# Score products of a transformer block on one Trainium2 core: 64-row tile pairs in every step with fillers

## The chip, the cores and the metric

The kernel runs on one core of one Trainium2 chip. The metric is the device time of one execution in microseconds (us); lower is better. A core has five engines that each work through their own instruction queue in order: PE (TensorE, matrix products into PSUM), DVE (VectorE), ACT (ScalarE), POOL (GpSimd) and SP (SyncE, which here only issues DMAs). They meet through semaphores.

## What is computed

One transformer block over 2048 rows of width 512, in bf16: layer norm, attention with 32 heads of width 16, a residual, layer norm, a gated feed-forward layer of width 1792, a residual.

```python
B, S, D, H, F = 1, 2048, 512, 32, 1792
q, k, v = split_heads(layernorm(x) @ wqkv)          # Dh = 16
p = softmax(einsum("bhqd,bhkd->bhqk", q, k) * Dh ** -0.5)
h = x + merge_heads(einsum("bhqk,bhkd->bhqd", p, v)) @ wo
g, u = layernorm(h) @ w_gate, layernorm(h) @ w_up
out = h + (sigmoid(g) * u) @ w_down
```

## The kernel before

**Tiling.** Queries are cut into five chunks, three of 512 and two of 256 (`CHUNKS`, L43). Within a chunk `c`, heads go in eight groups `g` of four heads `j`. A unit (`units`, L390) is one head against one bank's worth of keys: 128 keys by 512 queries, or twice 128 keys by 256 queries in the last two chunks. Three units in a row make a step (`groups`, L391, `GU = 3`); there are 683 steps `i`. Four steps are a cycle (`CYC = 4`); below, "step 0 to 3 of a cycle" is `i % 4`.

**A step.** `emit_scores(i)` (L746) issues the step's score products on PE into one of two PSUM buffers of three banks, `pss2[i % 2]`: three matmuls with 512 columns, or six with 256. Then ACT takes the exponential of the three tiles in one instruction (L776) and writes it to SBUF. In a split step (`split`, L898: step 0 of each cycle, and step 2 of the cycles that are in `twice`, L899 to L905) ACT takes two tiles and DVE the third, by a chain of a bit conversion that reads PSUM (`exp_bits`, L795) and four more operations in the steps that follow (L798 to L808). Scores of step `i` must wait until ACT, and DVE in a split step, have read the same buffer in step `i - 2`.

**What else PE does in a step.** After the scores stand, in this order: the products of exponentials with values that are due (`emit_pv`, L839: 12 matmuls of 17 columns of weights, most often in step 2 of a cycle), work put off by `later` (the normalisation by the row sums, loads), and then the fillers. Fillers are the other matrix products of the block (projections, output projection, feed-forward), written as one generator `filler` (L724) from which `emit_fill` (L861) takes a number of matmuls each step: `rate` (L737) allows 2 to 3 of full size in steps 0, 1 and 3 of a cycle, none where values are due. Fillers also pause: a `yield ("gap", n)` or `("at", n)` in the generator sets `state["wait"]`, the step at which they go on, to leave time for the DVE or ACT work on their result. The order on every engine is this program order.

**Two ways to write a score product.** `KT` holds 128 rows for a group of four heads: 32 rows a head, of which 16 carry the keys and the other 16 carry ones for a bound. `QB` (per head) is zero outside the head's own rows. So a product over all 128 rows gives one head's scores, and so does a product over the 64 rows in which the head lies (heads 0 and 1 in rows 0 to 63, heads 2 and 3 in rows 64 to 127). With `pairs` the 64 rows are used, with a tile position (L764 to L767); two such matmuls in different halves can run in PE side by side. Where the first two units of a step lie in the same half, `order` (L753, L754) turns the second and third round, so that the first two matmuls always lie in different halves; the third stands alone.

**Who has pairs now.** All steps before step 44 (`FIRST`); after that the odd steps, and all four steps of a cycle in `twice`. `idle` (L750) marks steps 0 and 1 of a cycle, from step 132 on, in a stretch in which the fillers are finished or wait past the next cycle; those steps have no pairs.

Of the kernel before, what the change touches and what calls it, by code (L numbers as in the profile page):

```python
# [18 lines left out]
def kernel(  # L19
# [27 lines left out]
    CYC = 4  # L47
    RATES = ((2.0, 2.0, 0.0, 3.0), (2.0, 2.5, 0.0, 3.0))
    FIRST = 44
# [165 lines left out]
    def emit_q_rows(n):  # L215
        c, g = qgs[n]
        q0, w = CHUNKS[c]
        assert ("q", q0 // QC, g // 2) in ready
        for j in range(4):
            r = 64 * (g % 2) + DH * j  # L220
            nc.sync.dma_start(out=QB[n % 2][32 * j:32 * j + 32:2, j, 0:w],
                              in_=QTu[r:r + DH, g // 2, q0:q0 + w])

    def emit_q_bound(n, engs=(nc.sync, nc.sync)):
        c, g = qgs[n]
        q0, w = CHUNKS[c]
        qc, o = q0 // QC, q0 % QC
        assert ("b", qc, g // 2) in ready
        r = 32 * qc + 4 * g
        for h in range(2):  # L230
            engs[h].dma_start(out=QB[n % 2][64 * h + 1:64 * h + 2, 2 * h:2 * h + 2, 0:w],
                              in_=bnd[r + 2 * h:r + 2 * h + 2, o:o + w])
# [151 lines left out]
    def per_bank(c):  # L384
        return QC // CHUNKS[c][1]
# [360 lines left out]
    def emit_scores(i):  # L746
        group = groups[i]
        n = len(group)
        pss = pss2[i % 2]
        idle = i >= 3 * FIRST and i % CYC < 2 and (state["done"] or state["wait"] > i + CYC)  # L750
        pairs = i < FIRST or (i % 2 == 1 or i - i % CYC + 2 in twice) and not idle
        order = list(enumerate(group))
        if pairs and group[0][3] // 2 == group[1][3] // 2:  # L753
            order[1:] = order[:0:-1]  # L754
        n_of = max(per_bank(u[0]) for u in group)
        parts = [(ui, u, h) for h in range(n_of) for ui, u in order[:2] if h < per_bank(u[0])]
        parts += [(ui, u, h) for ui, u in order[2:] for h in range(per_bank(u[0]))]
        for ui, (c, g, k, j), h in parts:
            n_qg = c * NG + g
            w = CHUNKS[c][1]  # L760
            kt = k * per_bank(c) + h
            assert ("k", g // 2) in ready
            h0 = 64 * (j // 2)
            rows = slice(h0, h0 + 64) if pairs else slice(0, P)  # L764
            nc.tensor.matmul(pss[:, ui, h * w:(h + 1) * w], lhsT=KT[rows, g, kt * P:(kt + 1) * P],  # L765
                             rhs=QB[n_qg % 2][rows, j, 0:w], start=True, stop=True,
                             tile_position=(h0, 0) if pairs else None)  # L767
        for c, g, k, j in group:
            n_qg = c * NG + g
            if k == (12 if per_bank(c) == 1 else 0) and j == 3 and n_qg + 1 < len(qgs):  # L770
                emit_q_rows(n_qg + 1)
                emit_q_bound(n_qg + 1)
        slot = i % 7
        pt = pt4[slot] if slot < 4 else (pt_early if i < GM else pt_late)[slot - 4]
        na = n - 1 if i in split else n
        ex = nc.scalar.activation(out=pt[:, 0:na, :], in_=pss[:, 0:na, :], func=ACT.Exp, scale=DH ** -0.5 / QS)  # L776
        if na < n:
            scratch = scratch_of(i)
            tc.declare_no_dep(exp_bits(pss[:, na, :], *scratch).ins, ex.ins,
                              reason="both only read, from different banks")  # L780
            later(i + 1, lambda: exp_first(*scratch))
            later(i + 2, lambda: exp_second(*scratch))
            later(i + 3, lambda: exp_third(pt[:, na, :], *scratch))
        for ui, u in enumerate(group):
            p_of[u] = pt[:, ui, :]

    def scratch_of(i):
        if i % CYC:
            flat = OT[(int((i - 20) / SPC) + 1) % 2][:].rearrange("p g q -> p (g q)")
            return (flat[:, 0:2 * QC].bitcast(mybir.dt.int32), flat[:, 2 * QC:4 * QC].bitcast(mybir.dt.int32),  # L790
                    flat[:, 4 * QC:6 * QC].bitcast(FP32))
        return early_scratch if i < GM else late_scratch

    def exp_bits(src, e_bits, e_man, e_pol):
        return nc.vector.tensor_scalar(out=e_bits, in0=src, scalar1=ONE_BITS, scalar2=0.0, op0=ALU.add, op1=ALU.max)  # L795

    def exp_first(e_bits, e_man, e_pol):
        nc.vector.tensor_scalar(out=e_man, in0=e_bits, scalar1=0x7FFFFF, scalar2=-0x40800000,  # L798
                                op0=ALU.bitwise_and, op1=ALU.bitwise_or)
        m = e_man.bitcast(FP32)  # L800
        nc.vector.scalar_tensor_tensor(out=e_pol, in0=m, scalar=PA, in1=m, op0=ALU.add, op1=ALU.mult)  # L801

    def exp_second(e_bits, e_man, e_pol):
        nc.vector.scalar_tensor_tensor(out=e_pol, in0=e_pol, scalar=PB, in1=e_man.bitcast(FP32),  # L804
                                       op0=ALU.add, op1=ALU.mult)

    def exp_third(dst, e_bits, e_man, e_pol):
        nc.vector.scalar_tensor_tensor(out=dst, in0=e_pol, scalar=PC, in1=e_bits.bitcast(FP32),  # L808
                                       op0=ALU.add, op1=ALU.mult)
# [44 lines left out]
    def later(i, fn):  # L854
        due.setdefault(i, []).append(fn)
# [43 lines left out]
    twice = set()  # L899
# [24 lines left out]
    with tc.manual_schedule():  # L924
# [17 lines left out]
        for i in range(NS + LAG):  # L942
            if i < NS:
                emit_scores(i)
            for u in pv_due.pop(i, []):
                emit_pv(*u[:3], i)
            for fn in due.pop(i, []):
                fn()
            if 1 <= i < NS:
                emit_fill(i)  # L950
# [37 lines left out]
```

## Time and profile before

| | |
|---|---|
| median of 3 runs | 966.58 us (966.09 to 969.06) |
| the profiled execution, its own time | 967.7 us |
| its span, first to last instruction | 965.9 us |
| mean granted PE clock in it | 0.996 of full speed |
| ACT busy | 897.1 us (93%) |
| PE busy | 837.0 us (87%), 6409 matmuls |
| DVE busy | 788.7 us (82%) |
| exponentials on ACT (L776) | 683 instructions, 882.8 us |
| score products (L765) | 2560 matmuls, 473.2 us |

A group row reads: line, engine, operation, output<-inputs, partitions by elements and type, count | busy time, mean ns of one | idle time of the engine just before, with what ended it. For matmuls "64\*128" is the rows and columns of the weights. Matmuls are pipelined and their ends are modelled, so starts are the better measure of PE: what one matmul costs is the time to the start of the next.

The timeline reads: start, length, engine, line, operation, and how many instructions are merged in the row; in brackets the idle time before it and what ended it. A row of three merged matmuls lasts until the modelled end of the third. The windows view gives, for a stretch of the span, the busy time of an engine, the granted PE clock (1.00 is full speed) and DMA.

### The profile page before, as it was taken

The page shows a single profiled execution, that of the slowest core. Times are in us where ns is not written, and L with a number is a line of the kernel's source. Part 1 is how long each engine was busy: PE and PEld are TensorE (multiplying, and loading weights), DVE is VectorE, ACT ScalarE, POOL GpSimd, SP SyncE. Part 2 cuts the span into 40 slices and gives each one's busy share as a digit, 9 for nine tenths or more (in the row PEclk, how much of TensorE's full clock was granted, in tenths as well). Part 3 has the DMA queues.
Part 4 walks back from the last instruction along what each step waited for, and adds up shares of the span by engine and source line. Part 5 has one row for each costly group of instructions (what it writes and reads, how often), then busy time and mean ns, then how long its engine had stood idle before and what let it go on. Part 6 is the DMA issues. An engine that isn't in the chain of part 4 may idle for free.

```text
span 965.9 us, 17209 instructions
## 1 busy us (share of the span) xinstructions
PE 837.0 (87%) x6409; PEld 334.2 (35%) x6409; DVE 788.7 (82%) x1423; ACT 897.1 (93%) x770; POOL 39.0 (4%) x45
## 2 busy tenths in 40 slices
PE   4888888888889899988789999988788999998988
PEld 2221222222223232222222233222255555456646
DVE  8389999888888888898888888888898788777653
ACT  4799999999999999999999999989998999899862
POOL 4600000000000000000000000000000000000000
PEclk9999999999999999999999999999999999999999
DMA  5002341000003000001000000000010000110010
GB/s 161 20 1 56 114 95 38 15 15 3 15 26 103 15 15 16 16 12 27 15 26 27 16 16 16 12 17 26 16 29 24 16 12 13 27 32 16 9 35 12
DMA packets 37357, 28.39 MB, mean 29 GB/s; under 512 B 17692, under 2 KB 32632, under 8 KB 37272
## 3 DMA queue, kind: packets, MB, share of 16 engines
q1 hardware_dynamic: 35684, 25.71, 10.1%
q10 hardware_dynamic: 1588, 1.58, 0.5%
q8 instruction: 50, 0.82, 0.4%
q14 instruction: 35, 0.29, 0.1%
HBM read 20.31 MB, written 2.61 MB: 24 GB/s over the span
## 4 chain that ended last, share of the span: by engine, by line
PE 41%; DVE 26%; ACT 24%; issue 6%; DMA 2%; SPq 0%; ACTq 0%; DVEq 0%; POOL 0%
PE pss L765 20%; ACT pt L776 13%; PE acc L846 8%; PE pm L514 6%; ACT stg L776 4%; ACT wd L776 4%; DVE stg L795 3%; PE pm L530 3%; ACT QTu L776 2%; PE pm L490 2%; DVE st L137 2%; DVE reg L798 2%; DVE pt L808 2%; DVE y L801 2%; DVE y L804 2%
## 5 line engine op out<-in xcount | busy, mean ns | idle before, releaser
L765 PE MATMUL pss<-QB,KT 64*128 64x512 bf16 (+3 forms) x2560 | 473.2, 338 | 85.7 <-ACT pt L776 40.1
L776 ACT ACTIVATE pt<-pss 128x1536 bf16<-128x1536 f32 (+1 forms) x392 | 500.4, 1360 | 18.1 <-PE pss L765 14.8
L765 PEld LDWEIGHTS <-KT 64*128 64x128 bf16 (+1 forms) x2560 | 179.0, 95 | 345.4 <-issue 235.2
L776 ACT ACTIVATE stg<-pss 128x1536 bf16<-128x1536 f32 (+1 forms) x140 | 183.1, 1356 | 5.0 <-PE pss L765 4.2
L795 DVE TENSOR_SCALAR stg<-pss 128x512 int32<-128x512 f32 x123 | 84.8, 689 | 72.4 <-PE pss L765 60.5
L846 PE MATMUL acc<-pt,Vaug 128*17 128x512 bf16 (+1 forms) x1471 | 112.8, 339 | 5.8 <-DVE xs_all L820 3.7
L776 ACT ACTIVATE wd<-pss 128x1536 bf16<-128x1536 f32 (+1 forms) x80 | 103.8, 1392 | 1.4 <-PE pss L765 1.3
L776 ACT ACTIVATE QTu<-pss 128x1024 bf16<-128x1024 f32 (+1 forms) x71 | 95.5, 1345 | 1.7 <-PE pss L765 1.2
L801 DVE SCALAR_TENSOR_TENSOR y<-reg 128x512 f32<-128x512 f32 x123 | 85.2, 692 | 4.2
L804 DVE SCALAR_TENSOR_TENSOR y<-y,reg 128x512 f32<-128x512 f32 x123 | 84.2, 685 | 1.1
L846 PEld LDWEIGHTS <-Vaug 128*17 128x17 bf16 x2560 | 50.4, 89 | 97.4 <-issue 82.6
L530 PE MATMUL pm<-wd,reg 128*128 128x512 bf16 x224 | 62.4, 385 | 2.3 <-DVE ob L535 1.8
L514 PE MATMUL pm<-reg,reg 128*128 128x512 bf16 (+1 forms) x280 | 58.0, 337 | 6.4 <-DVE reg L527 6.2
L514 PE MATMUL pm<-reg,wu 128*128 128x512 bf16 (+1 forms) x280 | 58.1, 338 | 1.5 <-ACT sg L519 1.2
L798 DVE TENSOR_SCALAR reg<-stg 128x512 int32<-128x512 int32 x123 | 52.0, 423 | 2.0
L144 POOL TENSOR_TENSOR rs<-ve,pw_neg 128x1 f32<-128x1 f32 (+1 forms) x24 | 16.5, 687 | 894.5 <-DVE ve L142 893.9
L846 PE MATMUL acc<-stg,Vaug 128*17 128x256 bf16 (+1 forms) x564 | 50.7, 326 | 0.8 <-DVE stg L808 0.4
L527 DVE SCALAR_TENSOR_TENSOR reg<-sg,pm 128x512 bf16<-128x512 f32 x56 | 38.2, 683 | 14.5 <-PE pm L514 13.8
L808 DVE SCALAR_TENSOR_TENSOR pt<-y,stg 128x512 bf16<-128x512 f32 x70 | 47.8, 683 | 1.8
L519 ACT ACTIVATE sg<-pm 128x512 f32<-128x512 f32 x56 | 35.5, 633 | 10.3 <-PE pm L514 10.0
L795 DVE TENSOR_SCALAR wd<-pss 128x512 int32<-128x512 f32 x45 | 30.9, 687 | 13.0 <-PE pss L765 12.7
L163 PE MATMUL pm<-reg 128*128 128x512 bf16 x124 | 37.1, 387 | 1.2 <-DVE km L171 0.7
(115 smaller groups left out, 707.0 us busy)
## 6 DMA issues: line engine op xcount, KB each, us to landing
rb_all<-rd SPq DMA_DIRECT2D x96, 64.0 KB
reg<-in_A_x_dram SPq DMA_DIRECT2D x8, 256.0 KB
xr<-in_A_x_dram SPq DMA_DIRECT2D x16, 128.0 KB
out_dram<-ob SPq DMA_DIRECT2D x16, 128.0 KB
rb_all<-rd SPq DMA_DIRECT2D x60, 32.0 KB
KT<-stg SPq DMA_DIRECT2D x7, 256.0 KB
reg<-in_B_w_gate_dram SPq DMA_DIRECT2D x4, 448.0 KB
wu<-in_B_w_up_dram SPq DMA_DIRECT2D x4, 448.0 KB
```

The lines of the kernel that those rows point to most:

```text
L163: nc.tensor.matmul(ps[:], lhsT=wqkv_sb[:, c, w0:w0 + P], rhs=xnT[:, c, n * QC:(n + 1) * QC], start=(c == 0), stop=(c == DC - 1))
L514: nc.tensor.matmul(ps[:, i * w:(i + 1) * w], lhsT=wt[:, c, f * P:(f + 1) * P], rhs=hnT[:, c, 0:w], start=(c == 0), stop=(c == DC - 1))
L527: nc.vector.scalar_tensor_tensor(out=out, in0=a, scalar=1.0, in1=b, op0=ALU.add, op1=ALU.mult)
L530: nc.tensor.matmul(ps[:], lhsT=hT[:, f, tt * P:(tt + 1) * P], rhs=wd[:, f, :], start=(f == 0), stop=(f == FC - 1))
L765: nc.tensor.matmul(pss[:, ui, h * w:(h + 1) * w], lhsT=KT[rows, g, kt * P:(kt + 1) * P], rhs=QB[n_qg % 2][rows, j, 0:w], start=True, stop= ...
L776: ex = nc.scalar.activation(out=pt[:, 0:na, :], in_=pss[:, 0:na, :], func=ACT.Exp, scale=DH ** -0.5 / QS)
L795: return nc.vector.tensor_scalar(out=e_bits, in0=src, scalar1=ONE_BITS, scalar2=0.0, op0=ALU.add, op1=ALU.max)
L798: nc.vector.tensor_scalar(out=e_man, in0=e_bits, scalar1=0x7FFFFF, scalar2=-0x40800000, op0=ALU.bitwise_and, op1=ALU.bitwise_or)
L801: nc.vector.scalar_tensor_tensor(out=e_pol, in0=m, scalar=PA, in1=m, op0=ALU.add, op1=ALU.mult)
L804: nc.vector.scalar_tensor_tensor(out=e_pol, in0=e_pol, scalar=PB, in1=e_man.bitcast(FP32), op0=ALU.add, op1=ALU.mult)
L808: nc.vector.scalar_tensor_tensor(out=dst, in0=e_pol, scalar=PC, in1=e_bits.bitcast(FP32), op0=ALU.add, op1=ALU.mult)
L846: nc.tensor.matmul(acc[32 * j:32 * j + VW, 0:w], lhsT=Vaug[:, kt, 4 * g + j, :], rhs=p[:, h * w:(h + 1) * w], start=(kt == 0), stop=(kt == ...
```

## The change

One condition in `emit_scores` is changed. Before, a step from 44 on has pairs if it is odd or its cycle is in `twice`, and it isn't idle. After, every step has pairs that isn't idle.

```diff
         idle = i >= 3 * FIRST and i % CYC < 2 and (state["done"] or state["wait"] > i + CYC)
-        pairs = i < FIRST or (i % 2 == 1 or i - i % CYC + 2 in twice) and not idle
+        pairs = i < FIRST or not idle
         order = list(enumerate(group))
         if pairs and group[0][3] // 2 == group[1][3] // 2:
             order[1:] = order[:0:-1]
...
             rows = slice(h0, h0 + 64) if pairs else slice(0, P)
             nc.tensor.matmul(pss[:, ui, h * w:(h + 1) * w], lhsT=KT[rows, g, kt * P:(kt + 1) * P],
                              rhs=QB[n_qg % 2][rows, j, 0:w], start=True, stop=True,
                              tile_position=(h0, 0) if pairs else None)
```

It reaches 266 of the 683 steps: 129 that are step 0 of a cycle and 137 that are step 2. The 24 idle steps (12 of step 0, 12 of step 1) stay as they are. The number of instructions on each engine, the step in which each filler stands and the queues of ACT, DVE, POOL and SP stay the same; on PE the score matmuls of these steps change form, and some of them change places within their step.

## The prediction, made before the changed kernel was run

> **What bounds the kernel now.** I read the head of the page first, then ACT's groups by form, then what waits for the score line, then the timeline of single steps, last the granted clock.
>
> ```profile
> span 965.9 us, 17209 instructions
> PE 837.0 (87%) x6409; PEld 334.2 (35%) x6409; DVE 788.7 (82%) x1423; ACT 897.1 (93%) x770; POOL 39.0 (4%) x45
> ```
>
> ```profile
> L776 ACT ACTIVATE pt<-pss 128x1536 bf16<-128x1536 f32 x281 | 400.3, 1479 | 12.0 <-PE pss L765 9.2 <-issue 1.2 <-DVE y L801 0.6
> L776 ACT ACTIVATE stg<-pss 128x1536 bf16<-128x1536 f32 x100 | 144.4, 1477 | 3.6 <-PE pss L765 3.1 <-ACT pt L776 0.2
> L776 ACT ACTIVATE pt<-pss 128x1024 bf16<-128x1024 f32 x111 | 117.5, 1058 | 6.1 <-PE pss L765 5.6
> ```
>
> ```profile
> who waited for it (us, times):
>   DVE stg L795: 60.5, 59
>   ACT pt L776: 14.8, 29
> ```
>
> ACT is the bound: its chain of exponentials fills the span from 36 to 933 us. In the timeline two exponentials of 1536 that follow each other without delay start 1.331 us apart (the records overlap by some 0.12), and after one of 1024 the next starts 0.905 later. What PE can win is only what ACT waits for it. I went through the timeline and took, for every exponential from step 44 on, how much later it starts than 0.11 us before the end of ACT's instruction ahead of it; counting delays over 0.06 us, 95 exponentials are late by 30.0 us together: 31 of unpaired step 0 by 10.8 us, 23 of unpaired step 2 by 6.2, 31 of step 1 by 10.3, ten others by 2.7. Of the 10.8, one delay alone is 2.8 (below).
>
> **The price of a pair.** The timeline around 402 us has both forms between fillers:
>
> ```profile
> 402.43 0.81 PE L765 MATMUL pss<-QB,KT 128*128 128x512 bf16 x3
> 403.08 0.59 PE L530 MATMUL pm<-wd,reg 128*128 128x512 bf16 x2
> 403.60 0.61 PE L765 MATMUL pss<-QB,KT 64*128 64x512 bf16 x3
> ...
> 406.45 0.82 PE L530 MATMUL pm<-wd,reg 128*128 128x512 bf16 x3
> 407.20 0.60 PE L765 MATMUL pss<-QB,KT 64*128 64x512 bf16 x3
> 407.74 0.39 PE L530 MATMUL pm<-wd,reg 128*128 128x512 bf16 x1
> ```
>
> Unpaired scores hold PE for 403.08 - 402.43 = 0.65 us, three slots of 0.216. Paired they take two slots, since the first two matmuls start 3 to 4 ns apart. But the last filler ahead of them holds PE for 403.60 - 403.08 - 0.216 = 0.30 us instead of 0.216 (over the trace the median is 0.312), and the last score matmul ahead of a filler holds it for 0.308 (407.74 - 407.20 = 0.54 = 0.23 + 0.31). So each change between 128-row, 64-row and 17-column forms costs about 0.093 us. Between 256-column matmuls it is the same: 0.109 becomes 0.202 to 0.205.
>
> The 266 changed steps each lose one slot, 0.215 us (0.204 in the 76 with six matmuls of 256 columns): -56.3 us of PE time. The form changes follow from PE's neighbours. Step 0: 44 have fillers on both sides (+2 each), 59 fillers ahead and paired scores behind (+1 - 1), 21 paired scores on both sides (-2), the other five come out at 0. Step 2, always followed by value products: 97 have a filler ahead (+1), 40 paired scores (-1). Sum 88 - 42 + 97 - 40 = +103, x 0.093 = +9.6 us. PE is relieved of 46.7 us, most of which turns into PE's own waiting.
>
> For a step's own scores: they are ready 0.215 - 0.093 = 0.12 us earlier behind fillers (200 steps) and 0.31 earlier behind scores (64). Steps 0 and 2 follow an exponential of 1.331, while buffer release to exponential takes an unpaired step 0.05 + 0.43 + 0.47 = 0.95 us, so nothing is won where PE was free.
>
> **What of it reaches ACT.** From each late exponential I went back along PE until PE was idle, summing what the change takes off or adds on the way, no more than the delay. Unpaired step 0 gets back 3.9 us, step 2 3.6, step 1 0.7: 8.2 us, the lower bound; it lets every wait at which a walk ends stand. The upper bound comes from the 42 steps 0 and 2 of cycles in `twice`, paired already: late by 0.34 us together, 8 ns each. If all 266 became like these, the 17.0 us of steps 0 and 2 would shrink to 2.1; without the 2.8 that is 12.1. I take **-10 us**. The other delays hang on fillers that wait for DVE (step 1 of the last two chunks) and stay. ACT, DVE, SP and POOL have the same queues, no wait is added, and no step's DMAs move.
>
> **The clock.** The price on the other side is in the granted clock.
>
> ```profile
> 644.27:647.68 3.41, 2.27 (x13) 1.00 0.02 5
> 647.68:651.10 3.42, 3.13 (x14) 0.54 0.02 4
> ```
>
> ```profile
> 646.40 0.61 PE L765 MATMUL pss<-QB,KT 64*128 64x512 bf16 x3 [0.27 <-ACT stg L776]
> ...
> 647.97 1.03 PE L846 MATMUL acc<-pt,Vaug 128*17 128x512 bf16 x8 [0.96 <-DVE xs_all L820]
> ...
> 648.93 1.46 PE L530 MATMUL pm<-wd,reg 128*128 128x512 bf16 x3
> 650.19 1.40 PE L765 MATMUL pss<-QB,KT 128*128 128x512 bf16 x3
> ...
> 651.69 5.09 ACT L776 ACTIVATE pt<-pss 128x1024 bf16<-128x1024 f32 x4 [2.65 <-PE pss L765]
> ```
>
> From 647.7 us the clock was halved for 3.41 us (three fillers take 1.26 instead of 0.65) and ACT stood for 2.65. The other halving inside the kernel starts at 36.7 us, 179 times 3.413 earlier: so the clock is judged in fixed stretches of 3.41 us. I counted in each how long any matmul streams (columns x 0.42 ns from its start, overlaps once). The stretch ahead of 647.7 had 41%; all the others between 40 and 930 us that did not bring a halving had 45% or more. So the limit lies between. The change takes 0.215 us, 6% of such a stretch, out for every changed step in it. The thin places are steps 3, 0, 1 without fillers:
>
> ```profile
> 195.38 0.81 PE L765 MATMUL pss<-QB,KT 128*128 128x512 bf16 x3 [0.58 <-ACT pt L776]
> 196.73 0.61 PE L765 MATMUL pss<-QB,KT 64*128 64x512 bf16 x3 [0.54 <-ACT wd L776]
> 197.65 0.81 PE L765 MATMUL pss<-QB,KT 128*128 128x512 bf16 x3 [0.31 <-ACT wd L776]
> 198.38 0.81 PE L846 MATMUL acc<-pt,Vaug 128*17 128x512 bf16 x9
> ```
>
> There 43% becomes 31%. Laying the 3.41 us grid at every phase over the trace, I count before 0.7 stretches under 41% and 2.7 under 45%, after 5.3 and 9.7: some 22 places, each hit in a quarter of the phases on average. I take **5 more halvings**.
>
> What does one cost? Here, halved from 197.65: scores take 0.43 more instead of 0.65 in all, so the step's exponential is still in time; the 12 value products take 1.3 and their form changes 0.19 each, so step 3's scores start near 200.2 instead of 199.14. Its exponential, due at 200.11, then comes 0.8 (clock back) to 1.3 us late. The halving seen cost 2.8, of which some 1.1 was the wait on L820. Bounds 0.8 and 2.8; most thin places are like this one, so 1.2 each: **+6 us**.
>
> [...]
>
> **Sum.** 967.7 - 10 + 6 = 963.7 against the profiled execution (span 965.9 and 1.8 around it). That one lies 1.1 above the median of the runs, and I carry the offset over: **962.6 us**.
>
> **Rivals.**
> - *The clock decides (slower).* The limit is at 45% or above, and a halving falls on fillers: 9 more at 1.7 (2.8 less 1.1) = 15.3, gain 8.2: 966.6 + 7.1 = 973.7. From 5 more at 1.7, or 7 at 1.2, the gain is gone. For it: the 31% places lie far under any limit, and value products follow them. Against: each place needs the grid to fall right.
> - *The clock stays.* Paired tiles may count as more work, and only a stretch without any matmul may bring a halving: 966.6 - 10 = 956.6. For it: in the first 44 steps, all paired, a stretch of 45% at 74 us brought none. Against: 647.7. [...]
> - *Little reaches ACT.* If the delays hang on DVE and the fillers' waits, walks gain some 3 us (a third of 8.2), the halvings 5: 966.6 + 2 = 968.6. For it: 22.6 of the 30 us come after 531 us, where fillers wait for DVE most. Against: the 42 paired steps.
> - That the change does not do what it says I leave out: the form is set on the matmul itself.
>
> **Chances.** Forecast 0.42 (own range 959 to 967), clock decides 0.28, clock stays 0.15, little reaches ACT 0.15. The range runs from 955 (gain 12.1, no halving) to 974. A measurement here tells about 0.3% (2.9 us) from no change. Faster than 963.7: 0.28 of the forecast and all of the clock that stays, 0.43. Within: 0.14 of the forecast, 0.11 of the third rival, 0.03 of the first, 0.28. Slower: 0.29.
>
> **What would show it.** Right: score rows of even steps in the 64-row form with 0.31 us at their edges; unpaired L765 only in idle steps; ACT's idle time on L765 down by a third or more; four to eight rows of clock near 0.5, mostly ahead of value products behind stretches without fillers, each with ACT late by about a microsecond. Wrong: no halving, or more than nine; ACT's instructions longer while two tiles write PSUM; delays of steps 0 and 2 unchanged.

## The result and the profile after

| | before | after |
|---|---|---|
| median of the runs | 966.81 us (966.09 to 970.78, 8 runs) | 977.27 us (969.57 to 982.88, 8 runs) |
| ratio of times | | 1.0101, 95% interval 1.0066 to 1.0136 |
| profiled execution, own time and span | 967.7 and 965.9 us | 979.0 and 977.2 us |
| mean granted PE clock, profiled execution | 0.996 | 0.970 |
| mean granted PE clock, 8 runs of after | | 0.965 to 0.982 |

The changed kernel is about 1% slower, and its runs differ from each other by 13 us, where those before differ by 5. The 962.6 us forecast, and the range up to 974, were wrong.

The head of the page after the change, and its row of the granted clock in 40 slices (tenths of full speed):

```profile
span 977.2 us, 17106 instructions
PE 812.0 (83%) x6313; PEld 282.7 (29%) x6409; DVE 789.4 (81%) x1423; ACT 897.1 (92%) x770; POOL 39.0 (4%) x45
...
PEclk9898999998989999999999999999999999999999
```

ACT is busy for the same 897.1 us, so its instructions did not get longer while two tiles write PSUM. (This trace lacks 96 of the 6409 matmul records, so PE's busy time can't be compared closely.) The new thing is the 8 in the clock row, in four slices. Before, the row was:

```profile
PEclk9999999999999999999999999999999999999999
```

ACT's groups by form, and what waits for the score line:

```profile
L776 ACT ACTIVATE pt<-pss 128x1536 bf16<-128x1536 f32 x281 | 401.0, 1483 | 18.9 <-PE pss L765 15.2 <-ACT pt L776 1.6 <-issue 1.1
L776 ACT ACTIVATE stg<-pss 128x1536 bf16<-128x1536 f32 x100 | 144.7, 1484 | 4.4 <-PE pss L765 3.0 <-ACT stg L776 0.7 <-ACT pt L776 0.3
```

```profile
who waited for it (us, times):
  DVE stg L795: 57.5, 58
  ACT pt L776: 21.4, 33
```

The exponentials wait 15.2 us for the scores in the first group where it was 9.2, though nearly all score products now have the cheaper form. The timeline shows that form, now in a step 0 between fillers:

```profile
406.64 0.81 PE L530 MATMUL pm<-wd,reg 128*128 128x512 bf16 x2 [0.59 <-DVE reg L527]
407.38 0.60 PE L765 MATMUL pss<-QB,KT 64*128 64x512 bf16 x3
407.91 0.61 PE L530 MATMUL pm<-wd,reg 128*128 128x512 bf16 x2
408.45 1.29 PE L765 MATMUL pss<-QB,KT 64*128 64x512 bf16 x6
```

From 407.38 to 407.91 the scores hold PE for 0.53 us, as forecast (0.23 + 0.31), where the 128-row form took 0.65; the fillers behind them for 0.54, two slots of 0.216 and 0.1 for the change of form.

Where the time went is seen in the windows view and the timeline around 240 us, in a stretch without fillers. Columns of the windows: stretch, its length, busy time and count of PE, PEld, DVE, ACT, POOL, then the granted clock. (The windows were laid some 0.2 us ahead of the recorded switches of the clock, hence 0.53 and 0.97 at the ends of the halving.)

```profile
235.20:238.65 3.45, 1.70 (x9) 0.39 (x8) 2.48 (x4) 3.45 (x4) 0.00 (x0) 1.00 0.00 0
238.65:242.07 3.42, 2.56 (x18) 0.65 (x19) 1.98 (x3) 3.42 (x3) 0.00 (x0) 0.53 0.01 2
242.07:245.48 3.41, 3.41 (x11) 0.47 (x11) 1.81 (x3) 1.53 (x3) 0.00 (x0) 0.50 0.03 5
245.48:248.89 3.41, 3.41 (x19) 0.59 (x20) 2.58 (x5) 2.46 (x3) 0.00 (x0) 0.50 0.03 2
248.89:252.30 3.41, 3.10 (x21) 0.82 (x23) 1.90 (x4) 3.38 (x3) 0.00 (x0) 0.97 0.31 84
```

```profile
238.15 0.59 PE L765 MATMUL pss<-QB,KT 64*128 64x512 bf16 x3 [0.31 <-ACT wd L776]
...
239.50 1.04 PE L765 MATMUL pss<-QB,KT 64*128 64x512 bf16 x3 [0.39 <-ACT wd L776]
240.46 1.02 PE L846 MATMUL acc<-pt,Vaug 128*17 128x512 bf16 x5
...
241.97 1.03 PE L765 MATMUL pss<-QB,KT 64*128 64x512 bf16 x3 [0.47 <-issue]
...
243.10 1.02 ACT L776 ACTIVATE pt<-pss 128x1024 bf16<-128x1024 f32 x1 [0.97 <-PE pss L765]
...
245.03 1.45 ACT L776 ACTIVATE pt<-pss 128x1536 bf16<-128x1536 f32 x1 [0.91 <-PE pss L765]
...
248.89 2.50 ACT L776 ACTIVATE wd<-pss 128x1536 bf16<-128x1536 f32 x2 [0.90 <-PE pss L765]
```

After a thin stretch (nine matmuls) the clock is halved for three stretches of 3.41 us, the scores' row grows from 0.59 to 1.04, and ACT stands three times for 0.9 us or a little more. In two of the halved stretches PE reads as busy for all of 3.41 us: the busy column alone would call this a full engine.

I took the delays of the exponentials apart once more, in the same way as in the prediction, from step 44 on:

| us of delay of the exponentials | before | after |
|---|---|---|
| in or up to 1.5 us behind a halved stretch | 2.8 (1 stretch of 3.41 us) | 17.5 (15 stretches in 12 groups, one of them before step 44) |
| elsewhere | 27.3 | 20.8 |

By this split the pairs did bring 6.5 us, and the clock took 14.7. The other 3 us of the 11.3 between the spans lie before step 44, in steps that are the same in both kernels: there the clock was halved at 37.5 us for two stretches (one before the change), and at 85.3 us for two. How much is halved differs from run to run, as the mean clock of 0.965 to 0.982 shows.

The runs say the same without a trace. Each comes with its mean clock, so the time at half clock is (1 - mean clock) x 2 x time (the clock records of both traces have 1.0 and 0.5 alone). Over the 8 runs after, the time grows by 0.37 us per halved us (correlation 0.96), over 24 runs before by 0.30 (0.93). Drawn out to no halving, this gives **957.7 us after and 965.8 before**: at full clock the change gains some 8.1 us. The 957.7 lies far from the runs, all of which have some 35 us or more at half clock, and its standard error is 2.2 us. On average after had 53.1 us at half clock and before 4.9, 14 stretches more, each worth 0.37 x 3.41 = 1.26 us.

### The profile page after: what moved, and what is told of

It reads as the page before. It is cut to its first block, busy times and chain, and to the rows that moved or that the text cites. A ratio compares the mean times of both kernels' runs of the same rounds, so it can differ in the third digit from the quotient of the medians.

```text
span 977.2 us, 17106 instructions
## 1 busy us (share of the span) xinstructions
PE 812.0 (83%) x6313; PEld 282.7 (29%) x6409; DVE 789.4 (81%) x1423; ACT 897.1 (92%) x770; POOL 39.0 (4%) x45
## 4 chain that ended last, share of the span: by engine, by line
PE 39%; DVE 27%; ACT 23%; issue 6%; DMA 2%; SPq 1%; ACTq 0%; POOL 0%; DVEq 0%
PE pss L765 18%; ACT pt L776 12%; PE acc L846 7%; PE pm L514 6%; ACT stg L776 4%; ACT wd L776 4%; DVE stg L795 3%; PE pm L530 3%; DVE pt L808 2%; ACT QTu L776 2%; DVE st L137 2%; DVE y L804 2%; DVE reg L798 2%; DVE y L801 1%; PE pm L490 1%
## 5 line engine op out<-in xcount | busy, mean ns | idle before, releaser
L765 PE MATMUL pss<-QB,KT 64*128 64x512 bf16 (+3 forms) x2555 | 425.5, 345 | 109.4 <-ACT pt L776 51.3
L765 PEld LDWEIGHTS <-KT 64*128 64x128 bf16 (+1 forms) x2560 | 128.0, 94 | 384.2 <-issue 311.5
L846 PE MATMUL acc<-pt,Vaug 128*17 128x512 bf16 (+1 forms) x1471 | 117.6, 350 | 6.5 <-DVE xs_all L820 3.3
L530 PE MATMUL pm<-wd,reg 128*128 128x512 bf16 x200 | 58.6, 388 | 5.9 <-issue 3.2
L514 PE MATMUL pm<-reg,reg 128*128 128x512 bf16 (+1 forms) x252 | 55.6, 333 | 8.8 <-DVE reg L527 6.7
L519 ACT ACTIVATE sg<-pm 128x512 f32<-128x512 f32 x56 | 36.3, 647 | 10.5 <-PE pm L514 10.5
L163 PE MATMUL pm<-reg 128*128 128x512 bf16 x106 | 35.4, 406 | 3.2 <-issue 1.7
```

The costliest lines, as they stand in the source:

```text
L514: nc.tensor.matmul(ps[:, i * w:(i + 1) * w], lhsT=wt[:, c, f * P:(f + 1) * P], rhs=hnT[:, c, 0:w], start=(c == 0), stop=(c == DC - 1))
L519: nc.scalar.activation(out=sg[:], in_=ps[:], func=ACT.Tanh, scale=0.5)
L530: nc.tensor.matmul(ps[:], lhsT=hT[:, f, tt * P:(tt + 1) * P], rhs=wd[:, f, :], start=(f == 0), stop=(f == FC - 1))
L846: nc.tensor.matmul(acc[32 * j:32 * j + VW, 0:w], lhsT=Vaug[:, kt, 4 * g + j, :], rhs=p[:, h * w:(h + 1) * w], start=(kt == 0), stop=(kt == ...
```

## The experiments

Theory "clock": pairs gain time, and lose more because PE then does too little in stretches without fillers. Main rival "form": pairs cost by themselves, by the 103 more changes of form or by two tiles writing PSUM at once. A later rival asks what the halvings go with. Each kernel ran beside the kernel before on the same chip; "at full clock" is the line through its own runs, drawn out to no halving, with a standard error of 0.3 to 1.3 us for the experiments. Some runs need no line: those with a clock of 1.000 took 965.6 to 966.6 us before, and 961.1 and 961.4 us in e6.

| run | median us | ratio to before, 95% interval | mean clock | us at half clock | us at full clock |
|---|---|---|---|---|---|
| before | 966.9 to 967.2 | | 0.997 | 5 to 6 | 965.8 to 966.0 |
| the change | 977.27 | 1.0101 (1.0066 to 1.0136) | 0.973 | 53.1 | 957.7 |
| e1 pairs but in 56 thin steps | 964.16 | 0.9968 (0.9953 to 0.9983) | 0.994 | 11.1 | 960.4 |
| e2 pairs added in these 56 alone | 973.76 | 1.0068 (1.0053 to 1.0083) | 0.988 | 23.4 | 966.7 |
| e3 pairs added in step 0 alone | 969.77 | 1.0029 (1.0018 to 1.0041) | 0.992 | 16.1 | 965.8 |
| e4 pairs added in step 2 alone | 965.43 | 0.9989 (0.9976 to 1.0002) | 0.994 | 11.1 | 962.7 |
| e5 third repeated in 56 thin steps | 971.14 | 1.0035 (1.0014 to 1.0056) | 0.985 | 30.0 | 962.0 |
| e6 pairs but in 79 thin steps | 964.12 | 0.9962 (0.9947 to 0.9977) | 0.995 | 9.5 | 961.1 |
| e10 third repeated in 79 | 969.14 | 1.0011 (0.9986 to 1.0035) | 0.989 | 20.9 | 962.1 |
| e9 third repeated in all 266 | 979.95 | 1.0128 (1.0094 to 1.0162) | 0.990 | 19.0 | 974.0 |
| e13 third twice in 128 rows, 56 | 964.63 | 0.9975 (0.9963 to 0.9987) | 0.995 | 10.3 | 962.4 |
| e14 third once in 128 rows, 56 | 969.48 | 1.0021 (1.0001 to 1.0041) | 0.987 | 26.2 | 959.3 |
| e16 pairs but in 105 thin steps | 963.49 | 0.9953 (0.9940 to 0.9965) | 0.997 | 5.4 | 961.9 |

**The two halves of the change by place.** "Thin" steps are even changed steps with no or almost no fillers in them and their neighbours (`THIN`, a list of step numbers taken from the order of the fillers).

```diff
-        pairs = i < FIRST or not idle
+        pairs = i < FIRST or not idle and i not in THIN          # e1
+        pairs = i < FIRST or ((i % 2 == 1 or i - i % CYC + 2 in twice) or i in THIN) and not idle   # e2
```

> Pairs in every non-idle step except 56 'thin' even steps (no or almost no fillers in the step and its neighbours), which keep the 128-row form as before; 210 of the 266 changed steps stay changed. Theory 'clock' (the loss is the halved clock in stretches where PE streams too little; the pairs themselves gain 6 to 8 us): at most 3 halved stretches of 3.41 us inside the steps, mean clock 0.99 or more, 957 to 964 us, faster than before. Rival 'form' (the 103 more form changes, or two tiles writing PSUM beside ACT's reads, cost time in every changed step): the loss of 10.5 us falls with the number of changed steps only, 210 / 266 x 10.5 = +8 us, about 975 us.

> The kernel before with pairs in those 56 thin even steps added and in no other. Theory 'clock': nearly all halved stretches of the changed kernel come back (8 to 15), mean clock 0.97 to 0.98, little of the gain since almost nothing waits in thin steps: 973 to 982 us. Rival 'form': 56 / 266 x 10.5 = +2 us, about 969 us, clock 0.99 or more.

e1 is faster than both kernels at a clock of 0.994, with 210 of the 266 steps changed (964.16; I had 957 to 964). e2 changes only 56 steps and loses 6.8 us; its trace has seven halved stretches. Its time is as I had expected, but its halvings are fewer (I had 8 to 15, and a clock of 0.97 to 0.98 where 0.988 was measured). The rival, by which the loss follows the number of changed steps, had +8 and +2 us: it falls. The two gains at full clock, 5.4 and -0.8 (the second no further from nothing than its error of 1.1), also say where the pairs pay: not in thin steps.

**The two halves by step.**

```diff
-        pairs = i < FIRST or not idle
+        pairs = i < FIRST or ((i % 2 == 1 or i - i % CYC + 2 in twice) or i % CYC == 0) and not idle   # e3
+        pairs = i < FIRST or ((i % 2 == 1 or i - i % CYC + 2 in twice) or i % CYC == 2) and not idle   # e4
```

> Pairs added in step 0 of each cycle alone (129 steps), step 2 as before. Theory 'clock': a stretch of steps 3, 0, 1 without fillers loses its one changed step here just as in the full change, so most halvings stay (6 to 12), half of the gain: 969 to 977 us. Rival 'form': 46 of the 103 more form changes are here, so about half of the loss, 972 us, and clock 0.99 or more.

> Pairs added in step 2 of each cycle alone (137 steps), step 0 as before. Theory 'clock': steps 3, 0, 1 keep their streaming, and a stretch with step 2 has the value products in it, so few halvings more (1 to 4), some 3 us gained: 962 to 968 us. Rival 'form': 57 of the 103 more form changes are here, about half of the loss, 972 us, and clock 0.99 or more.

Step 2 alone gains 3 us at full clock and loses half of it to the clock, so that no gain clear of the scatter is left; step 0 alone gains nothing at full clock and ends 2.8 us slower than before. For step 0 that is less of both than I had expected. Between fillers it wins a slot (0.216 us) and pays two changes of form (0.19), which may be why. Together the two have 27.2 us at half clock and the full change 53.1, so the halves do not simply add. One estimate for this: by the count of the last section, in which all halvings came after stretches with 37.9% or less, a stretch of 3.41 us with two changed steps comes that low more often than one with a single one. No run tests this by itself.

**What do the halvings go with?** If with the time for which PE streams, a thin step can be filled up with any matmul.

```diff
+        for h in range(per_bank(c) if i in THIN else 0):
+            kt = k * per_bank(c) + h
+            nc.tensor.matmul(pss[:, ui, h * w:(h + 1) * w], lhsT=KT[rows, g, kt * P:(kt + 1) * P],
+                             rhs=QB[n_qg % 2][rows, j, 0:w], start=True, stop=True, tile_position=(h0, 0))
```

> The changed kernel with pairs everywhere, and in the 56 thin even steps the third score matmul is issued a second time (same rows, same output), so PE streams as long there as in the kernel before. Theory 'clock, by streaming time': the halvings go as they went when these steps kept the 128-row form: mean clock 0.99 or more, 958 to 964 us. Rival 'clock, by the array's share' (a 64-row matmul alone counts half, so a repeat helps little): clock 0.975 to 0.985, 969 to 974 us. Rival 'form': pairs and form changes as in the changed kernel, so about 977 us whatever the clock.

> Pairs everywhere, with the third score matmul repeated in the 79 thin steps. Theory 'clock, by streaming time': 958 to 963 us, clock 0.994 or more, as with the 128-row form in these steps or a little under it. Rival 'array's share': clock under 0.985, 969 us or more.

> Pairs in every non-idle step except 79 thin even steps: the 56, and those steps 2 with no filler in the step ahead (the two halvings left in the first experiment stood at such steps). Theory 'clock': the mean clock rises from 0.994 to 0.996 or more and the gain of the other 187 steps stays: 960 to 963 us. Rival (those halvings come from the wait for the accumulator, not from the missing score slot): clock and time as in the first experiment, 964 us.

My main theory missed here. Filled up to the same three slots, the thin steps of e5 still lose the clock: 971.1 us at 0.985, which is what the rival by the array's share had. With 79 steps it is the same in kind: 969.1 with repeats (e10), 964.1 with the 128-row form (e6). The clock of e10, 0.989, is above what the rival had (under 0.985) and below the main theory's 0.994. e6 against e1 shows no gain beyond the scatter; I had expected 960 to 963, and its rival (964 at the same clock) is what came. The windows of e5, at steps 180 to 182, and its timeline:

```profile
265.93:269.35 3.42, 1.98 (x13) 1.00 0.08 22
269.35:272.76 3.41, 3.41 (x22) 0.53 0.26 72
```

```profile
269.10 0.62 PE L765 MATMUL pss<-QB,KT 64*128 64x512 bf16 x3 [0.31 <-ACT wd L780]
269.53 0.62 PE L770 MATMUL pss<-QB,KT 64*128 64x512 bf16 x1
270.08 1.45 PE L850 MATMUL acc<-pt,Vaug 128*17 128x512 bf16 x9
...
272.59 1.45 ACT L780 ACTIVATE pt<-pss 128x1536 bf16<-128x1536 f32 x1 [0.86 <-PE pss L765]
```

The repeat (L770) is there, and the clock halves all the same; the value products take nearly twice their time (1.45 us for nine, 0.82 at full clock) and ACT waits 0.86 us, as worked out in the prediction for such a place (0.8 to 1.3).

That left a new theory: the halvings go with area times time, rows x columns of the tiles in use. By it a 64-row matmul alone is half a slot, a pair one, a 128-row matmul one. The next two runs hold time and area apart: e13 is e5 with the third score matmul and its repeat in 128 rows (three slots of time, area 3 where e5 has 2); e14 has the third once in 128 rows (two slots of time as in the change, area 2 as in e5).

```diff
-            rows = slice(h0, h0 + 64) if pairs else slice(0, P)
+            full = not pairs or i in THIN and ui == order[2][0]; rows = slice(0, P) if full else slice(h0, h0 + 64)
...
-                             tile_position=(h0, 0) if pairs else None)
+                             tile_position=None if full else (h0, 0))
+        for h in range(per_bank(c) if i in THIN else 0):          # e13 alone
+            kt = k * per_bank(c) + h
+            nc.tensor.matmul(pss[:, ui, h * w:(h + 1) * w], lhsT=KT[rows, g, kt * P:(kt + 1) * P],
+                             rhs=QB[n_qg % 2][rows, j, 0:w], start=True, stop=True)
```

> As the run with the third score matmul repeated in 56 thin steps, but there the third and its repeat use all 128 rows (same product, same number of matmuls and columns, same three slots; area of the array times time is 1 + 1 + 1 slots instead of 1 + 0.5 + 0.5). Theory 'clock, by area' (what counts in a stretch is rows x columns of the tiles in use x time): as with these steps unpaired, mean clock 0.992 or more, 963 to 966 us. Rival 'clock, by streaming time': as with the 64-row repeat, clock 0.985, 971 us.

> Pairs everywhere; in the 56 thin steps the third score matmul uses all 128 rows and nothing is repeated: two slots of time, as in the changed kernel, and area 1 + 1 slots, as in the run with the 64-row repeat. Theory 'clock, by area': as that run, clock 0.983 to 0.987, 969 to 973 us. Rival 'clock, by streaming time': as the changed kernel, clock 0.973, 977 us.

e13 has the same matmuls as e5, in the same order and number, and is 6.5 us faster with a third of the time at half clock: 964.63 against 971.14. e14 gives 969.48 and 26.2 us at half clock, near e5's 30.0 and far from the 53.1 of the change. Both answers are area's, and streaming time has both wrong. The 64 rows that the 128-row form adds only multiply zeros of `QB`, and the time at half clock fell from 30.0 to 10.3 us all the same.

One rival these runs do not part from area. The third matmul in 128 rows between paired scores also adds changes of form, so streaming time plus 0.093 us for each such change would put e1, e13, e14 and e5 in the same order. The stretches of the traces speak against it: in the count of the last section, 106 stretches that did not halve lie under the highest that did by this measure, ten by area. Nor do the runs tell the rows of the weight loads from those of the matmuls, and columns they do not vary.

The same steps in e13, at full clock throughout this trace:

```profile
265.94 0.71 PE L765 MATMUL pss<-QB,KT 64*128 64x512 bf16 x3 [0.31 <-ACT wd L780]
266.50 0.38 PE L770 MATMUL pss<-QB,KT 128*128 128x512 bf16 x1
266.80 0.82 PE L850 MATMUL acc<-pt,Vaug 128*17 128x512 bf16 x9
267.08 5.10 ACT L780 ACTIVATE pt<-pss 128x1536 bf16<-128x1536 f32 x4
```

Four exponentials run through without a wait.

**The form changes alone.** With the third matmul repeated in all 266 changed steps, PE streams as long as before and pays the added form changes.

> Pairs everywhere, with the third score matmul repeated in all 266 changed steps: PE streams as long as in the kernel before in each of them, and only the 103 more form changes (9.6 us of PE time) are left of the change. Theory 'clock': no more halvings than before, the scores come no earlier than before, behind fillers 0.09 us later: 966 to 971 us, clock 0.994 or more. Rival 'form' (the loss of the changed kernel comes from the form changes or from two tiles writing at once): 977 us or more, clock at will.

This missed too: 979.95 us, 974.0 at full clock, 8 us over before. In its trace the delays outside halved stretches are 35.9 us, 8.6 more than before, at 9.6 us of PE time for 103 more form changes. So here the added time seems to come through to ACT nearly whole, where I had expected it to be mostly hidden; the other 4 to 5 us are clock. The rival is right about this kernel, that form changes are not free, but not about the change itself, which saves 56 us of slots for them. That all of the 8 us come from the form changes is worked out, not tested by itself.

**A version that beats both.** The thin list by looser limits (105 steps, eight of them before step 44, where all steps had pairs):

```diff
-        pairs = i < FIRST or not idle
+        pairs = not idle and i not in THIN
```

> Pairs in every non-idle step except 105 thin even steps, chosen by few fillers in the step and its neighbours, eight of them before step 44 (which all had pairs so far). Theory 'clock, by area': fewer places under the limit than with 79 (the steps 26 to 34, 50 to 68 and 88 lay under 40% by area there), mean clock 0.996 or more, the gain of the other steps stays: 960 to 963 us, faster than both kernels. Rival: the pairs of those steps are needed, exponentials come late in them: 964 us or more at the same clock.

963.49 us, 0.9953 of before, half a microsecond above the range that I had: 5.4 us at half clock, as little as before, and 4 us less at full clock. It is the fastest of the runs, though e1 and e6 lie within 0.7 us.

## Why the prediction was wrong

- **What bounds, and the price of a pair: right.** The slots (0.53 us for paired scores between fillers), 0.093 us for a change of form and ACT's unchanged 897.1 us are in the trace as forecast.
- **What reaches ACT ("I take -10 us"): right but for its size.** It is 8.1 us by the line drawn out to full clock (10 is within its error) and 6.5 us by the delays in the trace, so nearer to the lower bound, 8.2. The cycles in `twice`, from which the upper bound came, were no fair sample: outside halved stretches the delays of the changed steps fell from 14.3 to 6.8 us, not to 2.1.
- **The price of a halving ("so 1.2 each"): right.** 1.26 us per stretch over the runs after, and 17.5 us of delay for 15 stretches, 1.17 each, in the trace; the lines of the other kernels have 0.24 to 0.39 us per halved us, 0.8 to 1.3 per stretch.
- **The count of halvings ("I take 5 more halvings"): this step failed.** It was 14 more: (53.1 - 4.9) / 3.41. With 14 x 1.26 in the sum, 966.8 - 8.1 + 17.7 = 976.4 against 977.3 measured (gain, price and count come from one line through these runs, so this only shows that the terms add up). The fault lies where I counted "how long any matmul streams (columns x 0.42 ns from its start, overlaps once)". By that, a changed step loses one slot of three. By area it loses one and a half, 9.5% of a stretch and not 6%. Counting the trace of before again, by area and over all phases of the grid, with a limit put at 37.5% (an estimate from the count of the last section), gives 1.4 places before and about 11 with the change taken out of it, some ten more; and a halving can last: 15 stretches after came in 12 groups. Both together make some 12 of the 14; the rest is open; in this estimate a limit a little higher would give it. The prediction did hold the upper end of its own count, 9.7, and the rival built on it, 973.7; I gave it 0.28, and its nine more were still too few.
- **The rivals.** "The clock decides" is what happened. "The clock stays" said that paired tiles may count as more work; e13 against e5 (10.3 and 30.0 us at half clock) speaks for a lone 64-row matmul that counts as less. It also had halvings behind stretches without any matmul alone; the traces have them behind stretches with nine matmuls (after, 235.20) and thirteen (before, 644.27). Its sum, 956.6, lies near the 957.7 of the line, since both leave the halvings out. "Little reaches ACT" falls with the 957.7 at full clock.

## What to carry to other kernels

Making PE's work cheaper was no gain where PE already had slack (-0.8 us at full clock in e2, no more than its error), and the saved work was paid back at half clock just where work was thin: 53.1 us at half clock after the change, 4.9 before. Use the cheap form where PE is what the bound engine waits for, and the full-size form where nothing waits; here that selection turned +10.5 us into -3.6. When a kernel's runs scatter more than before, look at the mean granted clock of each run first, and draw the time out to full clock, as far as the runs come near it: it separates what a change does from what the clock does.

## What the runs showed of the hardware that I had not expected

- In these traces the halvings went with area times time, not with streaming time alone. In the 13 traces, take every stretch of 3.41 us at full clock that starts between 40 and 930 us, with its ends where the clock record has them: 3334, of which 46 were followed by half clock. Sum rows x columns of the tiles in use x streaming time as a share of the whole array, with the 17-column value products counted as tiles of 32 columns. All 46 had 37.9% or less; of the 3288 others the lowest had 34.4%, and ten lay under 37.9%. (Before and after alone: 505 stretches, 13 halvings, the same 37.9% and 34.4%, and five of the 492 others under 37.9%.) That lowest one (after, from 262.8 us) has lost a record: two weight loads of L163 stand in it and one matmul, and with the second it would have 40.6%. With the ends taken 0.05 us earlier it is the only exception: all 46 have 37.2% or less, all others 37.3% or more. By streaming time alone 84 of the others lay under the highest that halved (50%), and with 0.093 us added for each change of form 106 (58%). This is a measure found by trying several on these traces, for this kernel: how the clock is set, no run shows. That the rows in use matter is read from e13 and e14 together with this count; that columns do, from the count alone.
- A halved clock did not always come back after one stretch: of the 55 halved stretches, 9 were followed by another (in after one from 85.3 us, and two from 238.9). What decides it, no run here shows.
- In each of the traces of before and after, the halvings inside the steps start whole multiples of 3.413 us apart and last 3.413, 6.827 or 10.240 us, and they lie differently against the kernel: the first came 36.98 us after the first instruction before the change, 37.50 after. The runs after the change scatter over 13.3 us (969.6 to 982.9), those of e16, whose 105 thin steps have no pairs, over 2.1 (962.1 to 964.2); where the stretches fall on the kernel is the likely reason, and no run shows it by itself.
